# Values of the first two batches loaded as natural rows and spread by TensorE

## The chip, the cores and the metric

One core of a Trainium2 chip runs the whole program. The metric is the device time of one execution in microseconds. All times below are microseconds.

## The reference

A Longformer attention is followed by an MLP with a cosine gate.

```python
batch, n_heads, seq, head_dim = (8, 8, 576, 64)     # n_global = 8, window = 32
scores = scale * np.matmul(q, k.transpose(0, 1, 3, 2))
mask = (np.abs(pos[:, None] - pos[None, :]) <= 32) | is_global[:, None] | is_global[None, :]
attn = softmax(np.where(mask, scores, -1e9))
x = np.matmul(attn, v)          # then laid out as 4608 tokens x 512
h = x @ w_in                    # 512 -> 2048
g = h * np.cos(h)
out = g @ w_out                 # 2048 -> 512
```

## The kernel before, in words

**Attention.** The work unit is a pair of heads, 32 pairs in all (`pr`, four to a batch); two pairs make a half batch (`s`, 16 of them). The 576 queries of a head are cut into 11 blocks of 56. A block sees 8 global keys and 120 window keys, so keys and values of a block stand on 128 partitions. `kw` holds the keys of a pair by block, `qb` the queries (with the 8 global queries in front), `vw` the values: 128 partitions x 11 blocks x 2 heads x 65 (the 65th column is ones, and gives the sum of the softmax). Each has four buffers in rotation.

- `scores` (L441): 11 matmuls `st`, three PSUM tiles of the tag "s" (three buffers); ScalarE makes `e` = exp (L443), VectorE multiplies by the mask into `pm` (L444).
- `values` (L453): 22 matmuls into `pv`; VectorE forms reciprocals and writes `xn` (L464).
- `turn_x` (L476): six transposes `tx`; VectorE copies into `xT` (L479), the transposed input of the MLP. At a batch's last pair GpSimd copies the eight global columns into `xT` (L484).

**Where the operands come from.** Keys and queries of the first four half batches are loaded by `load_qk` (L260, GpSimd's queue) into `kn` and `qn`, turned by TensorE (L408, `t`) and copied into `kw` and `qb` (L415, L428). Later half batches are cast to float16 scratch in DRAM by `cast_half` (L249 for v, L253 for k and q, on GpSimd's queue), and k and q are read back transposed by `turn_half` (L265, L266, SyncE's queue) and copied on VectorE (L418, L431). The values of every half batch go through the scratch `v16`: `load_v` (L304 to L311, SyncE's queue) reads overlapping windows of 120 rows, 128 bytes each, into `vw`, and `load_vg` (L316) copies the eight global rows into each block. The global rows of k, q and v are gathered (L289, GpSimd's queue).

**The MLP.** Tokens are handled in nine tiles of 512. `one` does one of 16 slices of the first matmul of a tile (L492, four matmuls `ph`), the cosine on ScalarE (L495) and the product `g` on VectorE (L496). `two` does a quarter of one of four output blocks (L506, four matmuls `po`); after the fourth, `o` is copied (L511 or L513) and stored by SyncE (L515). A tile may start when `ready[0]` allows it, and outputs are held back by `outs_by[0]`.

**The order** is written out by hand; each engine runs its instructions in that order. `FRONT` covers the half batches 0 and 1 and the first scores of 2, `THIRD` the rest of half batch 2, and `ORDER` each later one. In them `s`, `p` and `x` are scores, values and turn_x, `k` and `q` the local keys and queries, `g` the global ones, `L` load_qk, `W` load_w_in (L596), `c` a cast of v, `v` load_v and load_vg, `n` a square sum on ScalarE, `G` the casts of a later half batch, held until this half's `xn` is there (L670), and `1` and `2` are one and two. A letter a, z, c or d after the step picks the pair 2s, 2s+1, 2s+2 or 2s+3. After each half batch SyncE gets `turn_half(s + 2)` and the value loads of the half batch s + 2. w_out is loaded on GpSimd's queue at the start of half batch 2 (L694).

Of the kernel before, what the change touches and what calls it, by code (L numbers as in the profile page):

```python
# [9 lines left out]
FP32 = mybir.dt.float32  # L10
# [29 lines left out]

ORDER = "sa0 sa1 sa2 2 2 2 sz0 2 sz1 sz2 pa 1 1 2 xa pz G 1 1 2 xz n 1 1 2 kc qc 1 kd qd 2 1"

THIRD = "1 1 pa 1 1 xa pz G 1 1 kc qc xz 1 1 kd qd 1 n 1"

FRONT = ("s0.0 s0.1 s0.2 s1.0 s1.1 s1.2 L2 c2 W1 k2 q2 p0 v4 g4 k3 q3 s2.0 s2.1 s2.2 x0 p1 v5 g5 W2 s3.0 s3.1 s3.2 x1 k4 q4 p2 L3 W3 g6 "
         "k5 q5 x2 p3 I c3 g7 x3 n0 s4.0 s4.1 s4.2 s5.0 s5.1 s5.2 v6 v7")
OK_ALL = float(P * (B * NP * 2 * BP + B))


# [5 lines left out]
def dview(ap, offset, *dims):  # L55

    return bass.AP(ap.tensor, ap.offset + offset, [list(d) for d in dims])
# [134 lines left out]
def kernel(  # L192
# [38 lines left out]
    v16 = dram.tile([B * H * S, D], FP16)  # L231


    NV = 4
    kT = [keep.tile([P, 2, KT], FP16, name=f"kT{i}") for i in range(2)]
    qT = [keep.tile([P, 2, QT], FP16, name=f"qT{i}") for i in range(2)]
# [19 lines left out]
    def load_qk(s):  # L256

        base = s * 4 * S * D
        for src, dst in ((k, kn[s % 2][KPAD : KPAD + S // RW]), (q, qn[s % 2][0 : S // RW])):
            nc.gpsimd.dma_start(dst.rearrange("x h r d -> x h (r d)"),  # L260
                                dview(src, base, (RW * D, S // RW), (S * D, 4), (1, RW * D)))
# [34 lines left out]
    def load_v(pr):  # L296


        b, h0 = pr // NP, 2 * (pr % NP)
        vt = vw[pr % NV]  # L300
        for h in range(2):
            lo, i0, i1 = (b * H + h0 + h) * S * D, 0, NB
            if pr == 0 and h == 0:
                nc.sync.dma_start(vt[G + 32 : P, 0, h, 0:D], dview(v16, 0, (D, W - 32), (1, D)))  # L304
                i0 = 1
            if pr % 2 and h:

                nc.sync.dma_start(vt[G : G + 104, NB - 2, h, 0:D], dview(v16, lo + 472 * D, (D, 104), (1, D)))
                nc.sync.dma_start(vt[G : G + 48, NB - 1, h, 0:D], dview(v16, lo + 528 * D, (D, 48), (1, D)))
                i1 = NB - 2  # L310
            nc.sync.dma_start(vt[G:P, i0:i1, h, 0:D],  # L311
                              dview(v16, lo + (QB * i0 - 32) * D, (D, W), (QB * D, i1 - i0), (1, D)))

    def load_vg(pr):
        for h in range(2):
# [67 lines left out]

    w_in16 = const.tile([P, NC, DFF], FP16)
    w_out16 = const.tile([P, NF, DM], FP16)
    xT = keep.tile([P, NC, NT + 40], FP16)

    r_all = keep.tile([P, B * NP, 2 * BP], FP32)
    x_sq = keep.tile([P, B * NP // 2], FP32)
# [4 lines left out]
    def globals_k(pr):  # L394
        nc.gpsimd.tensor_copy(kw[pr % NK][:, :, 0:G], view(kgT[:, pr], (0, NB), (1, G)))
# [199 lines left out]
    def load_w_in(c):  # L595
        nc.gpsimd.dma_start(w_in16[:, :, c * 512 : (c + 1) * 512],  # L596
                        moe_w_in[:, c * 512 : (c + 1) * 512].rearrange("(c p) n -> p c n", p=P))

    STEPS = {"s": scores, "p": values, "x": turn_x}
    with tc.manual_schedule():  # L600

        nc.vector.memset(pio2, pi / 2.0)
        nc.scalar.activation(x_sq[:, 0:1], pio2, AF.Exp)
        nc.vector.memset(kn[0], 0.0)
        nc.vector.memset(qn[0], 0.0)
        nc.gpsimd.iota(p_i, pattern=[[0, 1]], base=0, channel_multiplier=1)
        nc.gpsimd.memset(ident16, 1.0)
        cast_half(0, "v")
        cast_half(1, "v")
        load_qk(0)  # L610
        nc.gpsimd.affine_select(ident16, ident16, [[-1, P]], ALU.is_equal, 0.0, base=0, channel_multiplier=1)
        index_rows()
        gather(k, kg32, 0)
        gather(q, qg32, 0)
        nc.gpsimd.iota(kid_i, pattern=[[QB, NB]], base=-(G + 32), channel_multiplier=1)
        nc.gpsimd.iota(d_i, pattern=[[-1, C]], base=0, channel_multiplier=1)
        for t in (kn[1], qn[1], qb[2], qb[3]):
            nc.scalar.memzero(t.rearrange("p a b c -> p (a b c)"))
        for i in range(2):
            nc.vector.memset(qb[i], 0.0)  # L620
        load_qk(1)
        gather(v, vg32, 0)
        load_w_in(0)
        nc.vector.memset(vw[0][0:64, 0, 0], 0.0)
        for i in range(NV):
            nc.vector.memset(vw[i][:, NB - 2 :], 0.0)
            nc.vector.memset(vw[i][:, :, :, D : D + 1], 1.0)
        load_v(0)
        load_v(1)
        local_k(0)  # L630
        local_q(0)
        build_globals(0)
        globals_k(0)
        globals_q(0)
        build_mask()
        local_k(1)
        local_q(1)
        globals_k(1)
        globals_q(1)
        nc.scalar.copy(vg16[:, 0], vg32[:, 0])  # L640
        load_vg(0)
        load_vg(1)
        for pr in range(2, 4):
            load_v(pr)
            load_vg(pr)
            globals_k(pr)
            globals_q(pr)
        pv = ps.tile([P, 2, 512], FP32, tag="pv", bufs=1)
        nc.vector.memset(pv, 0.0)
        nc.vector.memset(view(pv[:, :, D : D + 1], (512, 2), (65, 6)), 1.0)  # L650

        def load_values(pr):
            load_v(pr)
            load_vg(pr)

        pool_idx = []

        def load_idx(_):
            pool_idx.extend(
                nc.values_load(gidx_row[0:1, 2 * g : 2 * g + 1], engines=[mybir.EngineType.Pool],  # L660
                               min_val=0, max_val=S - 1)
                for g in range(G))

        def globals_kq(pr):
            globals_k(pr)
            globals_q(pr)

        def casts(s):

            nc.gpsimd.tensor_copy(gate, xn_of[s][0:1, 1, 0, 0:1])  # L670
            for n in range(4, 2 * B):
                if s == n - 3:
                    cast_half(n, "vkq")
            if s == 4:
                for src, dst in ((k, kg32), (q, qg32), (v, vg32)):
                    gather(src, dst, 1)

        gate = keep.tile([1, 1], FP16)
        LOCAL = {"k": local_k, "q": local_q}
        OTHER = LOCAL | {"g": globals_kq, "L": load_qk, "W": load_w_in, "c": lambda s: cast_half(s, "v"), "v": load_values, "n": x_squares,  # L680
                 "I": load_idx}
        for step in FRONT.split():
            f = (STEPS | OTHER)[step[0]]
            f(*[int(x) for x in (step[1:] or "0").split(".")])
        ready[0], front[0] = 1, False
        for i in range(2):
            nc.vector.memset(kT[i][:, :, 0:KL], 0.0)
            nc.vector.memset(kT[i][:, :, KL + S :], 0.0)
            nc.vector.memset(qT[i][:, :, S:], 0.0)
        make_identity(nc, ident)  # L690
        nc.vector.memset(ones16, 1.0)
        for s in range(2, B * NP // 2):
            if s == 2:
                nc.gpsimd.dma_start(w_out16, moe_w_out.rearrange("(c p) n -> p c n", p=P))  # L694
                cast_half(4, "vkq")
            outs_by[0] = 4 * (s - 2) if s < 5 else 8 * (s - 3)
            for pr in (2 * s + 2, 2 * s + 3):
                if 8 <= pr < B * NP:
                    globals_kq(pr)
            for step in (THIRD if s == 2 else ORDER).split():  # L700
                if step == "1":
                    one()
                elif step == "2":
                    two()
                elif step == "n":
                    x_squares(s - 1)
                elif step == "G":
                    casts(s)
                elif step[0] in "cv":
                    OTHER[step[0]](int(step[1:]))  # L710
                else:
                    f, pr = (STEPS | LOCAL)[step[0]], 2 * s + "azcd".index(step[1])
                    if pr < B * NP:
                        f(pr, *[int(x) for x in step[2:]])
            if s % 2 == 1:
                ready[0] = s // 2 + 1 + (s // 2 == B - 1)
            if s < B * NP // 2 - 2:
                turn_half(s + 2)
                load_values(2 * s + 4)
                load_values(2 * s + 5)  # L720
            if s == 5:
                build_globals(1)
        x_squares(B * NP // 2 - 1)
        tail[0] = True
        for i in range(NTT * NF):
            one()
            two()
            if i in (3, 6, 9, 12):
                weight_norms(i // 3 - 1)
            if i in (0, 3, 6, 9):  # L730
                weight_squares(i // 3)
            if i == 14:
                count = finish_check()
            if i == 30:
                raise_flag(count)
        assert not outs_q
# [35 lines left out]
```

## Time and profile before

| | us |
|---|---|
| median of 3 runs | 391.77 (391.38 to 392.03) |
| profiled execution, its time | 392.95 |
| profiled execution, its span | 391.3 |
| TensorE matmuls busy | 328.0 (84%) |
| VectorE busy | 257.4 (66%) |
| ScalarE busy | 241.3 (62%) |
| GpSimd busy | 113.1 (29%) |

The span runs from the first to the last instruction of one profiled execution. Busy is the sum of an engine's instructions; matmuls are pipelined and their ends are modelled. The queue q1 is SyncE's, q0 GpSimd's; q1 moved 124509 packets and 27.89 MB, q0 63952 packets and 18.75 MB. A granted clock of 1.00 is TensorE's full speed. A row of a timeline gives start, length, engine, line, operation, output and inputs, and in brackets the idle time before it and what ended it.

### The profile page before, as it was taken

To read this page: it belongs to the slowest core of one execution; us is meant where nothing else is said; L and a number is where in the kernel's file an instruction comes from. 1 tells how busy PE (TensorE), PEld (TensorE's weight loads), DVE (VectorE), ACT (ScalarE), POOL (GpSimd) and SP (SyncE) were. 2 spreads that over 40 slices of the span, in tenths; PEclk is the share of its full clock that TensorE was granted. 3 is DMA by queue.
4 is the path that set the end of the run, shared out by engine and by line. 5 is a ranking of instruction groups with operands and counts; after the bars stand their busy time and mean duration, and the time that the engine had idled before them with its cause. 6 is when DMAs were issued, how large, how long until landed. Compare 5 with 4: busy or idle time off the path is not lost.

```text
span 391.3 us, 7371 instructions
## 1 busy us (share of the span) xinstructions
PE 328.0 (84%) x2678; PEld 173.4 (44%) x2678; DVE 257.4 (66%) x597; ACT 241.3 (62%) x354; POOL 113.1 (29%) x250
## 2 busy tenths in 40 slices
PE   0346249874987999999999999999999879999994
PEld 0245234442343455555555555555555334444441
DVE  5367246785386868878888887888888444544300
ACT  4456135984475686787767777786787866244310
POOL 7565116506055615072252516313000100000000
PEclk9999556999799999999999999999999999999999
DMA  5999999999999999999999999999930000010121
GB/s 86 144 112 196 188 87 129 202 162 152 146 118 188 115 169 131 158 167 153 169 134 202 134 158 173 135 189 111 153 72 30 27 2 27 29 54 28 55 80 60
DMA packets 188504, 47.18 MB, mean 121 GB/s; under 512 B 177005, under 2 KB 183405, under 8 KB 188205
## 3 DMA queue, kind: packets, MB, share of 16 engines
q1 hardware_dynamic: 124509, 27.89, 59.3%
q0 software_dynamic: 63952, 18.75, 48.7%
q8 instruction: 23, 0.38, 0.5%
q14 instruction: 20, 0.16, 0.2%
HBM read 47.73 MB, written 21.23 MB: 176 GB/s over the span
## 4 chain that ended last, share of the span: by engine, by line
PE 69%; DMA 15%; DVE 4%; ACT 3%; SPq 3%; issue 3%; POOL 2%; POOLq 0%; ACTq 0%; DVEq 0%
PE po L506 31%; PE ph L492 27%; DMA k<-in_k_dram 5%; PE st L441 4%; PE pv L453 4%; DMA qT<-q 3%; PE tx L476 3%; DMA kn<-in_k_dram 2%; DMA vw<-vg 2%; DMA vg<-in_v_dram,gidx_rows 2%; SPq L316 1%; ACT cos L495 1%; DVE g L496 1%; DVE xn L464 1%; PE pn L538 1%
## 5 line engine op out<-in xcount | busy, mean ns | idle before, releaser
L492 PE MATMUL ph<-xT,w_in 128*128 128x512 f16 x576 | 142.3, 384 | 8.1 <-DVE g L496 5.4
L506 PE MATMUL po<-w_out,g 128*128 128x512 f16 x576 | 142.5, 384 | 1.2 <-DVE o L513 1.0
L495 ACT ACTIVATE cos<-ph,pio 128x512 f16<-128x512 f32 x144 | 97.2, 686 | 67.5 <-PE ph L492 67.1
L496 DVE TENSOR_TENSOR g<-cos,ph 128x512 f16<-128x512 f16 x144 | 96.2, 685 | 52.5 <-ACT cos L495 50.3
L492 PEld LDWEIGHTS <-w_in 128*128 128x128 f16 x576 | 54.0, 98 | 70.0 <-issue 13.4
L506 PEld LDWEIGHTS <-g 128*128 128x128 f16 x576 | 55.9, 99 | 65.6 <-issue 4.3
L443 ACT ACTIVATE e<-st 128x512 f16<-128x512 f32 (+1 forms) x96 | 47.7, 562 | 26.9 <-PE st L441 19.6
L444 DVE TENSOR_TENSOR pm<-e,mask 128x512 f16<-128x512 f16 (+1 forms) x96 | 36.8, 403 | 23.6 <-ACT e L443 19.7
L670 POOL COPY gate<-xn 1x1 f16<-1x1 f16 x14 | 2.5, 179 | 144.5 <-DVE xn L464 144.5
L441 PE MATMUL st<-qb,kw 128*128 128x128 f16 x352 | 30.9, 237 | 11.5 <-POOL qb L400 8.9
L441 PEld LDWEIGHTS <-kw 128*128 128x128 f16 x352 | 26.1, 107 | 21.9 <-issue 8.8
L464 DVE TENSOR_TENSOR xn<-pv,r_all 128x768 f16<-128x768 f32 x32 | 30.7, 958 | 1.9
L453 PE MATMUL pv<-vw,pm 128*64 128x65 f16 x704 | 20.1, 204 | 13.9 <-DMA vw<-vg 13.9
L484 POOL COPY xT<-xg 128x4 f16 x64 | 20.7, 323 | 22.8 <-DVE xT L479 19.3
L253 POOL DMA_DIRECT2D q<-in_q_dram x12 | 26.1, 2179 | 0.0
L453 PEld LDWEIGHTS <-pm 128*64 128x64 f16 x704 | 16.3, 117 | 18.5 <-issue 8.8
L511 ACT COPY o<-po 128x512 f32<-128x512 f32 x18 | 10.5, 585 | 22.5 <-PE po L506 22.1
L431 DVE COPY qb<-qT 64x616 f16<-64x616 f16 x48 | 22.1, 460 | 3.3 <-DMA qT<-q 3.0
L525 ACT ACTIVATE sq<-xn 128x1536 f16<-128x1536 f16 x16 | 23.6, 1474 | 0.0
L415 ACT COPY kw<-t 128x1320 f16<-128x1320 f16 x8 | 10.1, 1256 | 20.4 <-PE t L408 20.4
L476 PE MATMUL tx<-ident,xn 128*128 128x128 f16 x192 | 17.0, 228 | 6.4 <-DVE xn L464 6.4
L513 DVE COPY o<-po 128x512 f32<-128x512 f32 x18 | 12.3, 685 | 12.5 <-PE po L506 12.0
(109 smaller groups left out, 267.2 us busy)
## 6 DMA issues: line engine op xcount, KB each, us to landing
out_dram<-o SPq DMA_DIRECT2D x36, 256.0 KB
vw<-v SPq DMA_DIRECT2D x47, 165.0 KB
v<-in_v_dram POOLq DMA_DIRECT2D x16, 288.0 KB
k<-in_k_dram POOLq DMA_DIRECT2D x12, 288.0 KB
q<-in_q_dram POOLq DMA_DIRECT2D x12, 288.0 KB
vw<-v SPq DMA_DIRECT2D x16, 135.0 KB
w_in<-in_moe_w_in_dram POOLq DMA_DIRECT2D x4, 512.0 KB
w_out<-in_moe_w_out_dram POOLq DMA_DIRECT2D x1, 2048.0 KB
```

The costliest lines, as they stand in the source:

```text
L253: nc.gpsimd.dma_start(dst[s].rearrange("t (h d) -> t h d", h=4), dview(src, base, (D, S), (S * D, 4), (1, D)))
L441: nc.tensor.matmul(st[:, j], kp[:, g0 + j], view(qp[:, g0 + j], (1, P)), start=True, stop=True)
L443: nc.scalar.activation(e[:, :n], st[:, :n], AF.Exp, scale=scale)
L444: nc.vector.tensor_tensor(view(pm[:, g0], (1, n * P)), view(e, (1, n * P)), view(mask[:, g0], (1, n * P)), ALU.mult)
L453: nc.tensor.matmul(pv[r0 : r0 + C, j // 6, c0 : c0 + 65], pm[:, j, h], vp[:, j, h], start=True, stop=True)
L464: nc.vector.tensor_tensor(view(xn, (384, 2), (D, 6), (1, D)), view(pv, (512, 2), (65, 6), (1, D)), view(rp, (6, 2), (1, 6), (0, D)), ALU.mult)
L476: nc.tensor.transpose(tx[:, n], xn[:, n], ident16)
L492: nc.tensor.matmul(ph, w_in16[:, j, f * P : (f + 1) * P], xT[:, j, t * TT : (t + 1) * TT], start=(j == 0), stop=(j == NC - 1))
L495: nc.scalar.activation(cos, ph, AF.Sin, bias=pio2)
L496: nc.vector.tensor_tensor(g16[:, f], cos, ph, ALU.mult)
L506: nc.tensor.matmul(po, g16[:, f, s * P : (s + 1) * P], w_out16[:, f], start=(f == 0), stop=(f == NF - 1))
L525: nc.scalar.activation(sq, view(xn, (1, 2 * BP * P)), AF.Square, accum_out=x_sq[:, s : s + 1])
```

## The change

For the pairs 0 to 7 (batches 0 and 1) `cast_half(.., "v")`, `load_v` and `load_vg` go. In their place `load_vn` reads a half batch's values in float32 rows, 112 rows x 4 heads to a transfer (six transfers on SyncE's queue), into `vn32`, which takes the two buffers of the tag "g" ahead of the MLP's use. `cast_vn` casts them to float16 into a part of `xT` that is not yet used. `spread` builds the blocks on TensorE: for each of the 11 blocks one matmul with `own` puts the global rows in place, and one or two with a 0/1 matrix `shift` put the window rows in place; the three PSUM tiles (tag "s") are copied into `vw` by ScalarE, VectorE and ScalarE. `hold(s)` is a copy of one element on GpSimd that waits for the last transfer of half batch s.

The orders change with it. In FRONT the loads and casts of v go, and `C` (cast_vn), `w` (spread) and `V` (hold) come in. `THIRD` takes the spreads of the pairs 4 to 7, `V3 W3 O`, where `O` loads w_out and casts half batch 4. The new `FOURTH` replaces `ORDER` for half batch 3: scores, values and turn_x first, then `R`, which lets the MLP's second tile start, then 11 ones and 12 twos. `outs_by[0]` is 16 up to half batch 4, in place of 0, 4 and 8. The opening issues load_qk(0) first on GpSimd's queue, and the gathers of v before load_qk(1).

```diff
-THIRD = "1 1 pa 1 1 xa pz G 1 1 kc qc xz 1 1 kd qd 1 n 1"
-
-FRONT = ("s0.0 s0.1 s0.2 s1.0 s1.1 s1.2 L2 c2 W1 k2 q2 p0 v4 g4 k3 q3 s2.0 s2.1 s2.2 x0 p1 v5 g5 W2 s3.0 s3.1 s3.2 x1 k4 q4 p2 L3 W3 g6 "
-         "k5 q5 x2 p3 I c3 g7 x3 n0 s4.0 s4.1 s4.2 s5.0 s5.1 s5.2 v6 v7")
+THIRD = "1 1 C2 w4 pa 1 w5 1 xa V3 W3 O pz kc qc 1 1 xz kd qd 1 C3 wc G 1 wd n 1 1"
+
+FOURTH = "sa0 sa1 sa2 sz0 sz1 sz2 pa 1 1 xa pz 1 1 G xz n R 2 1 2 1 2 1 2 1 2 1 2 1 2 1 2 kc qc 1 2 1 2 kd qd 1 2 1 2"
+
+FRONT = ("s0.0 s0.1 s0.2 k1 q1 C0 w0 s1.0 s1.1 s1.2 L2 p0 k2 q2 C1 w1 x0 s2.0 s2.1 s2.2 p1 g4 k3 q3 w2 W1 x1 s3.0 s3.1 s3.2 p2 L3 g5 w3 x2 k4 q4 p3 "
+         "g6 g7 I s4.0 s4.1 s4.2 x3 n0 k5 q5 V2 W2 s5.0 s5.1 s5.2")
...
+    def load_vn(s):
+        for i in range(NVT):
+            m = min(VT, S - VT * i)
+            nc.sync.dma_start(vn32[s // 2][0:m, s % 2 * 3 + i // 2, i % 2 * 256 : i % 2 * 256 + 256].rearrange("p (h d) -> p h d", h=4),
+                              dview(v, (s * 4 * S + VT * i) * D, (D, m), (S * D, 4), (1, D)))
+    def hold(s):
+        nc.gpsimd.tensor_copy(gate, vn32[s // 2][0:1, s % 2 * 3 + 2, 256:257])
+    def cast_vn(s):
+        old, new = vn32[s // 2][:, s % 2 * 3 : s % 2 * 3 + 3].rearrange("p a (b n) -> p (a b) n", b=2), vn16(s)
+        nc.vector.tensor_copy(new[0:VT, 0:3], old[0:VT, 0:3])
+        nc.scalar.copy(new[0:VT, 3 : NVT - 1], old[0:VT, 3 : NVT - 1])
+        m = S - VT * (NVT - 1)
+        nc.vector.tensor_copy(new[0:m, NVT - 1], old[0:m, NVT - 1])
+    def spread(pr):
+        new, h0 = vn16(pr // 2), 2 * (pr % 2) * D
+        for g0 in range(0, NB, 4):
+            n = min(4, NB - g0)
+            t = ps.tile([P, 4, P], FP32, tag="s", bufs=3)
+            for j in range(g0, g0 + n):
+                i = j // 2
+                parts = ((2, i), (3, i + 1)) if j % 2 else ((0, i), (1, i - 1))
+                nc.tensor.matmul(t[:, j - g0], own[:, pr], vg16[:, 0].rearrange("p h d -> p (h d)"), start=True, stop=False)
+                parts = [(a, x) for a, x in parts if x >= 0]
+                for a, x in parts:
+                    m = min(VT, S - VT * x)
+                    nc.tensor.matmul(t[:, j - g0], shift[0:m, a], new[0:m, x, h0 : h0 + 2 * D],
+                                     start=False, stop=(a, x) == parts[-1])
+            copy = nc.vector.tensor_copy if g0 == 4 else nc.scalar.copy
+            copy(vw[pr % NV][:, g0 : g0 + n, :, 0:D], t[:, 0:n].rearrange("p n (h d) -> p n h d", h=2))
...
-        cast_half(0, "v")
-        cast_half(1, "v")
         load_qk(0)
+        for s in range(2 * SB):
+            load_vn(s)
...
         gather(k, kg32, 0)
         gather(q, qg32, 0)
+        gather(v, vg32, 0)
...
+        load_qk(1)
...
+        build_shifts()
         for i in range(NV):
-            nc.vector.memset(vw[i][:, NB - 2 :], 0.0)
             nc.vector.memset(vw[i][:, :, :, D : D + 1], 1.0)
-        load_v(0)
-        load_v(1)
+        build_mask()
...
-            if s == 2:
-                nc.gpsimd.dma_start(w_out16, moe_w_out.rearrange("(c p) n -> p c n", p=P))
-                cast_half(4, "vkq")
-            outs_by[0] = 4 * (s - 2) if s < 5 else 8 * (s - 3)
+            outs_by[0] = 16 if s < 5 else 8 * (s - 3)
...
-            for step in (THIRD if s == 2 else ORDER).split():
+            for step in {2: THIRD, 3: FOURTH}.get(s, ORDER).split():
```

## The prediction

> **What bounds the kernel now.** I read the page's slices first, then busy time by stage, then the chain of waits, then single rows of TensorE. In the slices each digit is 9.8 us; PE is TensorE's busy share, PEclk its granted clock.
>
> ```profile
> PE   0346249874987999999999999999999879999994
> PEclk9999556999799999999999999999999999999999
> ```
>
> From slice 14 on TensorE is full; the loss lies ahead of about 138 us. By stage, cut where TensorE starts the scores of each half batch (columns: PE, PEld, DVE, ACT, POOL busy, PEclk, DMA share, GB/s):
>
> ```profile
> 0.00:23.20 23.20, 3.33 (x67) 2.71 (x68) 11.64 (x43) 10.37 (x16) 12.82 (x25) 1.00 1.12 123
> 23.20:60.00 36.80, 18.45 (x307) 15.91 (x307) 17.91 (x47) 17.25 (x28) 14.07 (x39) 0.70 1.17 141
> 60.00:75.60 15.60, 14.88 (x160) 7.27 (x160) 11.38 (x31) 10.84 (x16) 10.80 (x16) 0.83 1.40 181
> 75.60:95.60 20.00, 13.04 (x119) 6.71 (x118) 13.06 (x31) 14.14 (x21) 7.16 (x19) 1.00 1.77 154
> 95.60:116.30 20.70, 17.25 (x127) 8.18 (x128) 13.30 (x32) 11.39 (x18) 4.92 (x5) 0.84 1.25 132
> 116.30:137.20 20.90, 17.77 (x143) 9.00 (x143) 16.14 (x36) 13.48 (x21) 12.62 (x25) 1.00 1.56 151
> 137.20:308.00 170.80, 170.25 (x1427) 91.24 (x1427) 143.06 (x326) 130.11 (x195) 50.72 (x125) 1.00 1.35 140
> ```
>
> TensorE is idle 38 us before 60, 14.5 us between 60 and 137.2, and 0.55 us in the 171 us after. The chain of waits (start, length, what) names the cause:
>
> ```profile
> 2.62 9.37 DMA kn<-in_k_dram
> ...
> 13.64 9.05 DMA vg<-in_v_dram,gidx_rows
> ...
> 23.09 5.49 DMA vw<-vg
> ...
> 43.65 5.86 SPq L316
> 49.56 3.82 DMA vw<-vg
> ...
> 62.29 19.45 DMA k<-in_k_dram
> ...
> 84.07 10.46 DMA qT<-q
> ```
>
> Keys behind two value casts on GpSimd's queue; the gather of global values, which also holds GpSimd's qb copies and so the first scores; then the value blocks, queued on SyncE; then the keys of half 4, queued behind w_out; then their transposition. Last, what one 128x128 matmul costs at either clock:
>
> ```profile
> 23.20 2.69 PE L441 MATMUL st<-qb,kw 128*128 128x128 f16 x22 [4.80 <-POOL qb L400]
> ...
> 45.68 0.21 PE L453 MATMUL pv<-vw,pm 128*64 128x65 f16 x1 [8.42 <-DMA vw<-vg]
> ...
> 75.60 0.78 PE L441 MATMUL st<-qb,kw 128*128 128x128 f16 x11
> ```
>
> 122 ns each in the first row, 71 ns in the last: half and full clock.
>
> **Start, up to the first scores.** The two casts of v ahead of kn go (they and kn and qn, 288 KB each, filled q0 until about 14), so kn and qn are issued at about 2.1 and 3.1. Half the queue's bytes would bring kn at 7 to 8; 24 value loads on SyncE's queue (2.36 MB, 9216 packets of 256 B) run beside it, so I take 9 and 11, with 13 as the late bound (as long as before). Turning k and q and their copies (0.79, 1.26, 0.73, 0.67 in the rows at 12 to 16) end at 14. The gathers of v now stand ahead of load_qk(1), so vg isn't behind kn1 and qn1: issued by 12.2, landed at 15 in place of 22.8. VectorE has the mask (5.8 us of rows, 16.65 to 22.45) behind its memsets and the building of the 0/1 matrices (two memsets and five small copies, under 1.6 us by the 128x260 memset's 0.28 and copies of 0.2 to 0.3): free at about 14. First scores at 15.5 to 17; I take 16, was 23.2.
>
> **Values of pairs 0 to 3.** The block loads and vg loads go, with their 8.4 and 3.7 us stalls. Each spread adds 11+11+10 = 32 matmuls of 128x128: 32 x 122 = 3.9 us at half clock, 32 x 71 = 2.3 at full. ScalarE gets two PSUM copies (0.59 and 0.45, from the 512-wide copy at L511), VectorE one (0.69, as L513); per half batch a cast on VectorE (768 wide, about 0.6 by 616 in 0.49, plus 0.2) and one of 0.56 on ScalarE (as e). The loads of halves 0 and 1: by 29.8 ns a packet and engine (q1: 59.3% of 16 x 391.3 us over 124509 packets) 4608 packets take 8.6 us, twice that if time goes by bytes, so they land between 11 and 20; all four by 37. GpSimd waits for half 1 in hold(1), with w_in 0, globals 2 and 3 and load_qk(2) behind it: at the latest 20, and pair 2's scores come at about 33. Hidden.
>
> On TensorE's own order, at half clock: s0 1.35 and k1 q1 1.5 (to 18.9), wait for the cast of values (VectorE ends it at 19.8, ScalarE, behind kw and two qb copies, at 21.8), spread to 24, s1 1.35, p0 0.95, k2 q2 1.5, wait of 1.5 for the second cast, spread 0 to spread 1 10 us apart. Second spread done at 33. From there to the last scores of the opening TensorE needs 13.5 us at full clock (x 0.5, s 0.78, p 0.57, k and q 0.95, spread 2.3), 23 at half; VectorE 17.4 (pm 4 x 1.2, xn with its reciprocals 4 x 1.54, xT and xg 4 x 0.68, qb 3 x 0.8, spreads 2 x 0.69). I take VectorE plus 1.6 of gaps: first MLP matmul at 52, was 59.98: **-8.0**. Bounds 47.5 (TensorE alone) and 61 (below).
>
> The clock matters here. In this trace it is full at 36.5 after ten busy us (k turned in 0.50), half after the hole from 37.3 to 45.7, and full again at 65 after 5 us of unbroken work. The Trainium skill (TensorE: Matmul & The Clock Gate, Part 1: The HAM clock gate) says that about 3.4 us of sustained work release it and an idle window of that length throttles it again. The trace agrees within its 5 us slices, and by that rule the second spread would already run full and the opening would end about 1.5 us earlier.
>
> **From the first MLP matmul to half 6 (59.98 to 137.91: 77.9 us before).** The order shows the same MLP work by the end of half 5 (32 ins, 16 outs), but pulled forward: half 3 gets 15 ins and 12 outs, half 4 7 and 4, half 5 none.
> - Half 2: 15.6 + four spreads of 2.27 - 2.5 (5 us at clock 0.50 that would be warm) = 22.2.
> - Half 3: 27 units of 0.865 (L492, L506) + 3.1 of attention + 1.5 for GpSimd, whose gate, casts and eight xT copies took 6.3 us (87.1 to 93.4) against about 5 units ahead of tile 1's first matmul, + 1 = 28.9.
> - Half 4: 11 units, 3.1, and 2 of waits = 14.6. The transposition of half 5 now stands on SyncE's queue behind the third output, so issued at the end of half 3; at 10.5 us plus issue it lands when half 4 asks for it.
> - Half 5: only attention, so bound by its chain on VectorE: 1.8 to the first e (with a table load), 3.5 for six e and pm, twice 2.2 for xn and xT, 0.5 for the turn, 2 x 0.75 for the first kw and qb: 12.2.
> - Then half 6 starts partly at half clock. After the hole ahead of half 4 twelve po took 5.23 us (97.69) where they later take 2.59: 2.6 is the bound, and I take 1.7, since half 5 has short gaps and no one long hole.
>
> Sum 79.6: **+1.7**. Hidden: w_in 2 and 3 now stand ahead of w_out and the casts of half 4 on GpSimd's queue, all issued after the xT copies of batch 0, at 50.5 rather than 60.6. 1.05 MB more at 138 GB/s (2.69 MB in 19.45 us) is 7.6 us: k lands at about 80 (81.7 before), qT at 92; half 3 copies it at 96. That cover is 4 us; beyond it each us is lost. w_out comes at 74.5, first used at 82. The dropped vw memsets free VectorE before it has anything urgent: nothing.
>
> From half 6 on the orders agree. -8.0 + 1.7 = -6.3. The profiled run took 392.95 (span 391.3), 1.2 above the median 391.77; its sum is 386.7, the median's 385.5.
>
> **Rivals.**
> 1. *The opening is bound by TensorE at full clock*, and half 5's hole closes as VectorE runs ahead: first MLP at 47.5 and about 3 us less later: 391.8 - 12.5 - 1.3 = 378. For it: TensorE would be busy without holes; against: VectorE's 17.4 us.
> 2. *SyncE's queue gives it back.* turn_half(6) follows half 5's transposition and ten value loads. Before, one such cycle took 13.4 us (103.42 to 116.79) and once 19.3 (84.07 to 103.42). At 19.3 the transposes for half 6 land at 136 rather than 130, half 6 starts up to 5 us late: 390.5. Against it: the long cycle waited for an output at its end.
> 3. *Slower: the spreads keep TensorE at half clock and in step with the copies.* Scores and spreads share three PSUM buffers, so each spread waits for ScalarE and VectorE, which wait for scores. If all spreads stand 10 us apart as the first two do, the fourth ends at 54, and p3, s4, x3, k5 q5, s5 with their gaps at half clock bring the first MLP to 63; with 79.6 and a cold start of 1.5 half 6 begins at 144: 391.8 + 6.3 = 398. It decides where the first MLP comes later than about 58. For it: 8.5 us of half-clock work a pair; against: holes of 1.5 us only, where the clock rose at 23 to 36 with less work.
> 4. *It does nothing*: keys land no earlier beside the value loads and half 5 takes the rest: 391.8.
>
> **How the numbers follow.** A measurement tells about 0.2% (0.8 us) from no change. Forecast 0.50 (380 to 390 by 4 us either way in the opening), rival 1 0.20, rival 2 0.12, rival 3 0.15, rival 4 0.03. Faster: 0.50 + 0.20 + 0.10 = 0.80; same 0.03; slower 0.17. The range from 376 to 395 takes in forecast, rivals 2 and 4, most of 1 and the near part of 3.
>
> **What would show it.** First scores at 16, spread rows 71 ns from the third on, first ph matmul near 52, half 6's first st near 130, an empty half 5 with PEclk falling. Wrong if ph starts after 58, if st waits on kn, if vn loads end after 40, or if kw and qb copies of half 4 wait for DMA.

## Result: 4% slower, and the profile after

| | before | after |
|---|---|---|
| median | 391.9 (391.38 to 392.52, 4 runs) | 408.42 (405.10 to 408.59, 4 runs) |
| profiled execution, its time | 392.95 | 405.1 |
| profiled execution, its span | 391.3 | 403.4 |

The ratio is 1.0397, with a 95% interval from 1.035 to 1.0445. The forecast was 385.5, with a range from 376 to 395: both missed, and the sign with them. The profiled execution of the changed kernel is the fastest of its four, 3.3 us below the median.

The slices of the page of the changed kernel (each digit 10.1 us):

```profile
PE   0499579777998459999999999999999969999993
PEclk9999579889999859999999999999999999999998
```

TensorE is busy earlier than before, but from 50 to 100 us PE stays at 7 in four slices with the clock at 7 or 8 in three of them, and at 131 to 151 there is a second valley (4 and 5, clock 8 and 5). By stage, cut where TensorE starts the scores of each half batch, and at the first MLP matmul (columns: PE, PEld, DVE, ACT, POOL busy, PEclk, DMA share, GB/s):

```profile
0.00:16.62 16.62, 2.09 (x34) 1.53 (x35) 12.21 (x46) 7.99 (x13) 11.02 (x22) 1.00 0.87 138
16.62:50.30 33.68, 27.62 (x467) 23.68 (x466) 20.83 (x51) 24.13 (x40) 14.22 (x42) 0.88 0.70 113
50.30:81.34 31.04, 25.46 (x291) 17.50 (x290) 17.19 (x40) 17.22 (x27) 10.96 (x15) 0.86 1.51 177
81.34:115.72 34.38, 29.02 (x187) 13.79 (x186) 20.00 (x41) 19.31 (x30) 6.88 (x18) 0.95 0.68 64
115.72:133.11 17.39, 13.60 (x123) 6.94 (x122) 12.60 (x30) 12.71 (x20) 4.94 (x5) 1.00 1.04 129
133.11:146.72 13.61, 5.12 (x81) 3.89 (x81) 10.78 (x28) 6.57 (x14) 5.59 (x9) 0.66 1.52 138
146.72:165.84 19.12, 19.12 (x143) 9.96 (x143) 12.39 (x29) 10.98 (x17) 13.54 (x31) 0.88 1.46 154
```

PEclk reads 1.00 in the first 28 us, but the matmuls there have the lengths of half clock (two of the spread take 0.42 us at 27.50 and 0.28 at 28.43). The last five rows are the half batches 2 to 6. Set against the kernel before (its half 7 starts at 154.87):

| stage | before | forecast | after | after minus forecast |
|---|---|---|---|---|
| up to the first MLP matmul | 59.98 | 52.0 | 50.30 | -1.7 |
| half 2 | 15.6 | 22.2 | 31.0 | +8.8 |
| half 3 | 20.0 | 28.9 | 34.4 | +5.5 |
| half 4 | 20.7 | 14.6 | 17.4 | +2.8 |
| half 5 | 21.6 | 12.2 | 13.6 | +1.4 |
| half 6 | 17.0 | 18.7 | 19.1 | +0.4 |
| half 7 on | 236.4 | 236.4 | 237.6 | +1.2 |

(The forecast's 1.7 for a cold start stands in half 6.) So the gain of the opening came, and the halves 2 to 5 took back more. The chain of waits names other links than before (start, length, what):

```profile
11.36 4.81 DMA vg<-in_v_dram,gidx_rows
...
54.55 1.32 DVE xT L343
...
82.93 1.28 ACT L502
...
86.61 3.45 PE ph L551 x8
...
138.56 7.62 DMA vg<-in_v_dram,gidx_rows
```

Between 16 and 138 no DMA is left in it. New are the cast of values (L343), the eight ph matmuls of half 3 at half clock (3.45, where eight take 1.90 later), and the second gather of global values, which holds the first scores of half 6. In half 2 the rows of TensorE and VectorE show why the cast is there (lines of the changed kernel: L365 and L369 are the spread, L343 the cast on VectorE, L555 the product g):

```profile
50.30 2.87 PE L551 MATMUL ph<-xT,w_in 128*128 128x512 f16 x8
...
55.92 0.27 PE L369 MATMUL t<-xT 112*128 112x128 f16 x1 [2.70 <-DVE xT L343]
...
69.58 1.02 PE L551 MATMUL ph<-xT,w_in 128*128 128x512 f16 x4 [0.25 <-DVE g L555]
70.44 0.22 PE L365 MATMUL t<-vg,xT 128*128 128x128 f16 x1
72.91 0.27 PE L369 MATMUL t<-xT 112*128 112x128 f16 x1 [2.25 <-DVE xT L343]
...
73.39 0.42 PE L369 MATMUL t<-xT 112*128 112x128 f16 x2
```

```profile
53.35 1.28 DVE L555 TENSOR_TENSOR g<-cos,ph 128x512 f16<-128x512 f16 x2 [1.18 <-issue]
54.55 1.31 DVE L343 CAST xT<-vn 112x768 f16<-112x768 f32 x1
...
71.70 0.69 DVE L555 TENSOR_TENSOR g<-cos,ph 128x512 f16<-128x512 f16 x1
72.30 0.55 DVE L343 CAST xT<-vn 112x768 f16<-112x768 f32 x1
```

The order is `1 1 C2 w4`: the cast stands behind two products g, which wait for two cosines and a table load of ScalarE. TensorE, which has nothing between `w4` and the two ones, waits 2.70 us, then spreads at half clock (two matmuls in 0.42 us; at full clock 0.28). At `C3 wc` it waits 2.25 us: there the cast stands behind a copy of queries, which waits for ScalarE's copy, and a product g with its cosine; no table load is in the way. The first cast takes 1.31 us and the second 0.55; the last section shows what held the first.

### The profile page after: what moved, and what is told of

Read it like the earlier page. It is cut to its first block, busy times and chain, and to the rows that moved or that the text cites. A ratio compares the mean times of both kernels' runs of the same rounds, so it can differ in the third digit from the quotient of the medians.

```text
span 403.4 us, 7909 instructions
## 1 busy us (share of the span) xinstructions
PE 348.2 (86%) x2934; PEld 191.7 (48%) x2934; DVE 266.5 (66%) x615; ACT 249.6 (62%) x372; POOL 111.1 (28%) x249
## 4 chain that ended last, share of the span: by engine, by line
PE 71%; DVE 8%; ACT 7%; DMA 5%; issue 4%; POOL 4%; POOLq 0%; ACTq 0%; DVEq 0%
PE po L565 29%; PE ph L551 26%; PE st L500 5%; PE t L369 4%; DVE g L555 4%; PE pv L512 3%; DMA vg<-in_v_dram,gidx_rows 3%; ACT cos L554 2%; PE tx L535 2%; PE t L365 2%; DMA kn<-in_k_dram 2%; ACT e L502 2%; POOL q L257 1%; ACT qb L487 1%; DVE qb L487 1%
## 5 line engine op out<-in xcount | busy, mean ns | idle before, releaser
L551 PE MATMUL ph<-xT,w_in 128*128 128x512 f16 x576 | 143.8, 385 | 7.0 <-DVE g L555 5.0
L555 DVE TENSOR_TENSOR g<-cos,ph 128x512 f16<-128x512 f16 x144 | 96.4, 686 | 66.2 <-ACT cos L554 62.8
L502 ACT ACTIVATE e<-st 128x512 f16<-128x512 f32 (+1 forms) x96 | 47.7, 563 | 15.4 <-PE st L500 10.0
L523 DVE TENSOR_TENSOR xn<-pv,r_all 128x768 f16<-128x768 f32 x32 | 30.6, 958 | 1.9
L369 PE MATMUL t<-xT 112*128 112x128 f16 (+1 forms) x168 | 23.0, 255 | 5.7 <-DVE xT L343 5.2
L543 POOL COPY xT<-xg 128x4 f16 x64 | 19.7, 308 | 14.8 <-DVE xT L538 11.4
L535 PEld LDWEIGHTS <-xn 128*128 128x128 f16 x192 | 13.4, 102 | 14.7 <-DVE xn L523 9.1
L365 PE MATMUL t<-vg,xT 128*128 128x128 f16 x88 | 20.2, 255 | 0.0
```

Source lines behind the costliest of these rows:

```text
L365: nc.tensor.matmul(t[:, j - g0], own[:, pr], vg16[:, 0].rearrange("p h d -> p (h d)"), start=True, stop=False)
L369: nc.tensor.matmul(t[:, j - g0], shift[0:m, a], new[0:m, x, h0 : h0 + 2 * D], start=False, stop=(a, x) == parts[-1])
L502: nc.scalar.activation(e[:, :n], st[:, :n], AF.Exp, scale=scale)
L523: nc.vector.tensor_tensor(view(xn, (384, 2), (D, 6), (1, D)), view(pv, (512, 2), (65, 6), (1, D)), view(rp, (6, 2), (1, 6), (0, D)), ALU.mult)
L535: nc.tensor.transpose(tx[:, n], xn[:, n], ident16)
L551: nc.tensor.matmul(ph, w_in16[:, j, f * P : (f + 1) * P], xT[:, j, t * TT : (t + 1) * TT], start=(j == 0), stop=(j == NC - 1))
```

## Experiments

Each is compared with the kernel before, run on the same chip. "Half 2" is the time from the first MLP matmul to the first scores of half 3, the others from scores to scores; these lengths are from the one profiled execution of each run.

**1. The old order of half 3.** `FOURTH` and the early outputs are undone, the spreads stay.

```diff
-            outs_by[0] = 16 if s < 5 else 8 * (s - 3)
+            outs_by[0] = 4 * (s - 2) if s < 5 else 8 * (s - 3)
-            for step in {2: THIRD, 3: FOURTH}.get(s, ORDER).split():
+            for step in {2: THIRD}.get(s, ORDER).split():
```

> The changed kernel with the MLP's old order in half batch 3 (ORDER and the old outs_by in place of FOURTH). Theory A (the time is lost in half batch 2, to the spreads of pairs 4 to 7, the casts ahead of them and the half clock behind those waits): half 2 stays at 31 us, halves 3 to 5 together take about what they took before the change (62) in place of 65, so 403 to 408 us. Theory B (pulling the MLP forward empties half 5, and that hole is the loss): halves 3 to 5 fall to 50 to 55, so about 395 or less.

Measured: 394.48, ratio 1.0112 (1.007 to 1.0154). Halves 3 to 6 took 17.8, 19.4, 18.9, 17.0: 73.1 in all, where the changed kernel took 84.5 and the kernel before 79.3. The time is theory B's, though halves 3 to 5 took 56.1, a little more than its 50 to 55. So `FOURTH` and the early outputs cost 11.4 us of these halves. Without them the halves take 6 us less than before the change, behind a half 2 that is 18 us longer (33.6), which gives the transfers more time. Half 2 itself stayed long.

**2. No values for pairs 4 to 7.** The casts C2, C3 and the four spreads of half 2 are left out.

```diff
-THIRD = "1 1 C2 w4 pa 1 w5 1 xa V3 W3 O pz kc qc 1 1 xz kd qd 1 C3 wc G 1 wd n 1 1"
+THIRD = "1 1 pa 1 1 xa V3 W3 O pz kc qc 1 1 xz kd qd 1 G 1 n 1 1"
```

> The changed kernel without the casts and spreads of half batches 2 and 3: pairs 4 to 7 use the values that pairs 0 to 3 left in vw, so that part of the computation is left out. Theory A: half 2 falls from 31 to about 16 us as before the change, and half 3 loses some of its half clock: 390 to 394 us. Theory B: only the 9 us of matmuls of the four spreads go, the hole stays: 398 to 400.

Measured: 391.16, ratio 1.0035 (1.0003 to 1.0067). Half 2 fell from 31.0 to 16.0. Casts and spreads together cost 15 us there, more than the 9 us that four spreads take at full clock.

**3. The second gathers earlier.** GpSimd's six gathers go from half 4's casts to half 3's, so that half 6 need not wait for them.

```diff
+            if s == 3:
+                for src, dst in ((k, kg32), (q, qg32), (v, vg32)):
+                    gather(src, dst, 1)
...
-            if s == 4:
-                for src, dst in ((k, kg32), (q, qg32), (v, vg32)):
-                    gather(src, dst, 1)
```

> The changed kernel with the second set of gathered global rows issued one half batch earlier (ahead of the casts of half batch 6). Theory A: GpSimd's 6.4 us wait at 140 goes, and half 6 starts when its keys are copied, at about 141 to 143 in place of 146.7, with less half clock after it: minus 4 to 6 us, 402 to 404. Theory B says the same for this one or less (its hole is bound by VectorE's chain): minus 0 to 3.

Measured: 414.49, ratio 1.0625 (1.0584 to 1.0667): slower still. The gathers stood ahead of GpSimd's copies of the global columns of `xT`, which the MLP's second tile needs:

```profile
107.35 1.86 PE L551 MATMUL ph<-xT,w_in 128*128 128x512 f16 x4 [9.35 <-POOL xT L543]
```

Half 3 grew from 34.4 to 44.8, and after the wait four matmuls took 1.86 us, at half clock. Half 5 no longer ended on a gather, and was no shorter (14.3 against 13.6; half 6 then waited 3.42 us for the copies of `xT`), so taking the gather out of the end of half 5 did not shorten it. Neither theory had foreseen that the gathers would hold half 3.

**4. The casts earlier.** C2 and C3 go into FRONT, ahead of the MLP; spreads and `FOURTH` stay.

```diff
-... "1 1 C2 w4 pa 1 w5 1 xa ... 1 C3 wc G 1 wd n 1 1"
+... "1 1 w4 pa 1 w5 1 xa ... 1 wc G 1 wd n 1 1"
-... k4 q4 p3 g6 g7 ... k5 q5 V2 W2 ...
+... k4 q4 p3 C2 g6 g7 ... k5 q5 C3 V2 W2 ...
```

> The changed kernel with the casts of values of half batches 2 and 3 moved from half 2 into the opening, where VectorE and ScalarE wait for the keys (40 to 50 us). Theory A: TensorE's two waits of 2.7 and 2.3 us for the cast go, and with them the half clock of spreads 4 and 6 (1.6 us each): half 2 falls from 31 to 24 us, 400 to 402. Theory B: no more than the two waits, given back in half 5's hole: 405 to 408.

Measured: 398.7, ratio 1.0248 (1.0212 to 1.0284). Half 2 fell from 31.0 to 22.9, with a granted clock of 0.96 in place of 0.86, and the opening was no longer (49.7). So 8.2 us of half 2 came from the place of two casts. TensorE is idle there for 5.6 us in the changed kernel and for 0.6 in this one: 4.95 us are the two waits, and the other 3.2 are matmuls that ran slower.

**5. Both undone** (the edits of 1 and 4 together).

> The two that helped, together: the old MLP order in half 3 (e1) and the casts of values of half batches 2 and 3 in the opening (e4). Theory C (two losses that stand in different stages and add: about 8 us in half 2 to the casts' place with the half clock after it, about 11 in halves 3 to 6 to the pulled-forward MLP): half 2 takes 23, half 3 18, half 4 19.5, half 5 19, so half 6 starts at 129 in place of 138 and the time is 380 to 384. Rival D (they share one cause, the DMA queues, so that one gain takes the other's place): keys of half 4 are awaited again, 388 to 392.

Measured: 383.99, ratio 0.9842 (0.9808 to 0.9877). Half 2 took 22.9, halves 3 to 6 70.3. The place of the casts and the order of half 3 are enough to turn 4% slower into 1.6% faster.

**6. Two spreads earlier too.** To 5, the spreads of pairs 4 and 5 go into FRONT, behind p3 and k5 q5, with C2 behind w3.

```diff
-... g5 w3 x2 k4 q4 p3 C2 g6 g7 ... k5 q5 C3 V2 ...
+... g5 w3 C2 x2 k4 q4 p3 w4 g6 g7 ... k5 q5 w5 C3 V2 ...
```

> As e5, and the spreads of pairs 4 and 5 moved into the opening's two waits of TensorE for the queries' copies (2.2 us at 41, 2.7 us at 47). Theory C: half 2 falls by two spreads (4.5 us) to 18.5, the opening grows by at most 2: minus 2 to minus 4 against e5. Rival D: no change against e5, or slower, since the three PSUM buffers are shared with the scores.

Measured: 378.08 (376.95 to 380.59), ratio 0.9699 (0.9645 to 0.9752): it beats both kernels. The slices of its page (9.4 us each):

```profile
PE   0499969787898999999999999999999879999993
PEclk9999999999999999999999999999999999999997
```

From 27 us on the granted clock stays up, and the first MLP matmul comes no later (49.4), though two spreads more stand ahead of it: they fill gaps. Half 2 took 18.8.

**7. Spread for batch 0 only.** With the old order, batch 1's values again take the scratch: `SB = 1`, with `c2 v4 v5 c3 v6 v7` in FRONT.

> Spreads for batch 0 alone: the values of batch 1 come by casts to scratch, block loads and loads of global rows as before the change (four pairs), old MLP order in half 3. Theory C: half 2 takes 16 as before, if the loads of pairs 4 to 7 land while the opening runs; DMA between 20 and 60 us gets 1.4 MB in 128-byte packets, so the keys of half 4 land later than in e5: 382 to 388. Rival D: block loads are what held the opening, first MLP at 55 or later, 388 to 394.

Measured: 380.65, ratio 0.9738 (0.9695 to 0.9782). The opening's gain (first MLP matmul at 50.5) is kept without any spread in half 2 (15.4), but half 3 took 20.3, as in the kernel before, where run 6 takes 16.4.

**8. Experiment 2 with the old order** (pairs 4 to 7 without values, `ORDER` and `outs_by` as in 1).

> As e1, without the casts and spreads of half batches 2 and 3 (pairs 4 to 7 use the values that pairs 0 to 3 left in vw; that part of the computation is left out). The bound of what the place of those spreads can cost. Theory C: half 2 takes 16, and then the keys of half 4 (turned by about 84) are awaited by 2 to 4 us in half 3; half 6 starts at 122 to 126, 375 to 380. Rival D: the wait for the keys takes all that half 2 gives, 382 or more.

Measured: 380.81, ratio 0.9755 (0.9712 to 0.9798). With half 2 at 16.0, half 3 took 19.6 and half 4 20.1. This is slower than 6, in which four spreads more are done. What half 2 saves is waited for at the end of half 3, where VectorE needs the transposed queries of half 4:

```profile
84.57 0.95 DVE L490 COPY qb<-qT 64x616 f16<-64x616 f16 x2 [3.85 <-DMA qT<-q]
```

**9. The clock alone.** In the changed kernel TensorE gets 28 matmuls, overwritten by the spread, ahead of the spreads of pairs 4 and 6, so that it isn't idle while it waits for the casts.

```diff
+            if pr in (4, 6) and g0 == 0:
+                for _ in range(28):
+                    nc.tensor.matmul(t[:, 0], own[:, pr], vg16[:, 0].rearrange("p h d -> p (h d)"), start=True, stop=True)
```

> The changed kernel with 28 more matmuls of 128x128 ahead of the spreads of pairs 4 and 6; their sums are overwritten, they wait for nothing and stand where TensorE waits for the cast of values (2.7 and 2.3 us), so they add work and hide in the wait. Theory C1 (the half clock behind those waits is a good part of half 2's loss): PEclk in half 2 rises from 0.86 to over 0.95, half 2 takes 27 to 28.5 us in place of 31, 404 to 406 us. Rival C2 (the loss is the waits and the added copies themselves): half 2 stays at 31 to 33 and the time is unchanged or up to 2 us longer.

Measured: 404.1, ratio 1.0283 (1.0225 to 1.0341). Half 2 fell from 31.0 to 28.4, its clock rose to 0.93; some was given back (half 5 15.8). So keeping TensorE busy in the waits is worth about 2.6 us, most of the 3.2 that experiment 4 left to slower matmuls.

The other runs bear this out. With the two casts in half 2, its length goes with the number of 3.41 us stretches in which the clock is at half behind a wait for a cast: none in run 9 (28.4), one in run 16 (29.7), two in the changed kernel and in runs 3 and 11 (30.9 to 31.2), four in runs 1 and 13 (33.6). A stretch costs about 1.3 us.

**10. and 14. The queue's order without the spread.** Run 10 (kernel before, load_qk(0), the gathers of v and load_qk(1) moved up) gave 403.6, but says nothing on the question: load_qk(1) then stood ahead of ScalarE's clearing of its target, the clearing waited for the loads, and the first scores came at 30.6. (Half 1's keys and queries are cleared after their load in it, so it leaves out their part of the computation.)

> The kernel before, with block loads throughout; only the queue's order at the start is the changed kernel's: load_qk(0) ahead of the two casts of v, the gathers of v ahead of load_qk(1). Theory S (the opening's 9.7 us came from the values being on chip): first scores at 17 to 19, but the value blocks and global rows are awaited as before, first MLP matmul at 58 to 60, 389 to 392. Rival Q (it came from the queue's order): first MLP at 52 to 54, 383 to 386.

Run 14 leaves load_qk(1) behind the clearing:

```diff
+        load_qk(0)
         cast_half(0, "v")
         cast_half(1, "v")
-        load_qk(0)
...
         gather(q, qg32, 0)
+        gather(v, vg32, 0)
...
         load_qk(1)
-        gather(v, vg32, 0)
```

> The kernel before with only the order of GpSimd's queue from the change: load_qk(0) ahead of the two casts of v, and the gather of v right behind the gathers of k and q; load_qk(1) stays behind ScalarE's clearing. Values still go through the scratch, with no spread. Theory S (the spread brought the opening's gain): the value blocks still come late, first scores at 16 to 18 but pv waits for vw, first MLP matmul at 57 to 60, 389 to 392 us. Rival Q (the queue's order alone brought it): first scores at 16 to 18 and first MLP matmul at 52 to 54, 383 to 386 us.

Measured: 389.12, ratio 0.9968 (0.9933 to 1.0002). The scores start 4 us earlier than in the kernel before, the MLP doesn't:

```profile
19.10 2.69 PE L441 MATMUL st<-qb,kw 128*128 128x128 f16 x22 [3.55 <-POOL qb L400]
...
43.62 0.21 PE L453 MATMUL pv<-vw,pm 128*64 128x65 f16 x1 [6.47 <-DMA vw<-vg]
...
59.49 3.57 PE L492 MATMUL ph<-xT,w_in 128*128 128x512 f16 x8 [1.04 <-POOL xT L484]
```

The value blocks take nearly all of it back: 0.5 us is left of the opening's 9.7. So the queue's order alone did not bring them; the new path of the values did, with the order of `FRONT` that goes with it.

**11. Without `R`.** `FOURTH` without the step that lets tile 1 start in half 3, so that eight ins go to half 5.

> The changed kernel without the step R, so that the second MLP tile may start only after half 3: nine ins move from half 3 back into halves 4 and 5, all else stays (casts and spreads in half 2 too). Theory H (half 5's time is its attention chain, with TensorE idle 8.5 of 13.6 us, so MLP work put there is nearly free): half 3 falls by about 8 to 26 or 27, half 4 grows to 18 to 19, half 5 to 16 to 18, half 6 starts warm (17): 404 to 405 on the scale of 408.4. Rival K (half 3 is bound by waits, not by its 27 units): half 3 stays above 31, 408 or more.

Measured: 405.55, ratio 1.0344 (1.0281 to 1.0407). Half 3 fell to 26.6, and half 5 grew from 13.6 to 22.0: nothing won, where the expectation had half 5 at 16 to 18. An empty half 5 alone is thus not the cause.

**12. Two spreads in half 3.** To 6, the spreads of pairs 6 and 7 go from half 2 into half 3, behind the scores.

```diff
-... {2: THIRD}.get(s, ORDER)
+... {2: THIRD, 3: ORDER.replace('sa2', 'sa2 w6').replace('sz2', 'sz2 w7')}.get(s, ORDER)
```

> As e6, with the spreads of pairs 6 and 7 moved from half 2 into half 3, behind each pair's scores, where TensorE waits for the exponentials (half 3 had 3.5 us of idle TensorE in 16.4). Theory C: half 2 falls by about 4.5 to 14.3, half 3 grows by 2 to 3: minus 1.5 to 2.5 us against e6. Rival D: half 3 grows by all of it, since spreads and scores share three PSUM buffers: no change or slower.

Measured: 385.48, ratio 0.9822 (0.9756 to 0.9888), slower than 6. Half 2 gave 3.4 us, half 3 took 5.8 more, halves 4 and 5 together 4.4 more: rival D's result. That the shared buffers are the reason is not shown.

**13. and 16. Outputs held back; order alone.** 13 keeps `FOURTH` and `R` and takes the old `outs_by` (first line of 1). 16 also leaves out `R`, so that each half has the amounts of 1 in the order of `FOURTH`.

> The changed kernel with the old release of the outputs (outs_by 4, 8, 16) and FOURTH and R kept: half 3 has 15 ins and 4 outs in place of 15 and 12, half 4 the same 7 and 4, half 5 has 8 outs in place of none. Theory F (outs are the work that fills attention's waits, since they ask nothing of ScalarE and VectorE but one copy in four; spent early, half 5 stands without): half 3 34.4 - 8 x 0.865 = 27.5, half 5 17 or less with 8 outs where it took 13.6 with none, half 6 17 to 19; half 7 starts at 161 where it started at 165.8; 399 to 402 us. Rival W (each half has waits of its own, and outs only cost what they take wherever they stand): half 3 27.5, half 5 20.5, half 7 at 165 to 166; 405 to 408 us, as the changed kernel.

> e13 without the step R as well: FOURTH's order (attention of half 3 first, then the MLP), with the amounts of the old order in every half (half 3: 6 ins and 4 outs, half 4: 8 and 4, half 5: 8 and 8). So it differs from e1_order3 only in the order within half 3. Theory A (what counts is how much MLP work is pulled into half 3 and taken from half 5): as e1_order3, half 3 17 to 18.5, half 5 19, half 7 at 156; 394 to 396 us. Rival O (the order within half 3 counts: attention bunched at its front leaves its waits open): half 3 8.65 of units + 3.1 of attention + the 8 us that the changed kernel's half 3 loses = 19.8 to 22, half 7 at 159 to 161; 397 to 400 us.

Measured: 13 gave 399.97, ratio 1.0215 (1.0139 to 1.029), 16 gave 394.63, ratio 1.0127 (1.007 to 1.0184). Half 5 of 13, then of 16, and of 11 (columns as by stage above):

```profile
129.47:143.77 14.30, 10.90 (x113) 5.93 (x114) 11.45 (x27) 6.59 (x13) 10.21 (x17) 1.00 0.99 107
```
```profile
115.74:134.67 18.93, 17.41 (x145) 9.17 (x146) 16.89 (x36) 14.01 (x23) 10.67 (x18) 1.00 1.35 132
```
```profile
126.14:148.09 21.95, 14.32 (x112) 7.48 (x113) 16.51 (x33) 13.78 (x25) 11.34 (x21) 0.84 1.35 131
```

With the other runs they make a square:

| half 5 | no outs | 8 outs |
|---|---|---|
| no ins | 13.6 (after), 14.3 to 15.8 (runs 2, 3, 4, 9) | 14.3 (run 13) |
| 8 ins | 22.0 (run 11) | 18.9 (runs 1, 5 to 8, 14, 16), 21.6 to 21.9 (before, runs 10, 12) |

Run 11 and run 13 each stand alone in their cell. Eight outs are 6.9 us of matmuls. Put into a half without ins they lengthen it by 0.7 at most, and with them a half with ins is not longer than without, and up to 3.1 shorter. The granted clock is 1.00 with them (13, 16) and 0.66 (after) or 0.84 (11) without. Of the halves 3 to 6, the changed kernel takes 84.5, run 13 77.2, run 16 72.7, run 1 73.1. So of some 12 us, 7.3 go when the outs are held back, and 4.5 more when `R` goes too. Taken the other way round, `R` alone gives 0.4 (run 11 takes 84.1) and the outs then 11.4: the two losses do not add, and the early outs are the larger one by either way. The order of steps within half 3 costs nothing in sum (16 against 1): half 3 is 2.4 us longer in it (20.2 against 17.8), as rival O had it, but half 4 gives that back (16.6 against 19.4), so the time is theory A's.

## Why the prediction was wrong, step by step

**The opening: right in its number, and in part by luck.** First scores 16.62 (forecast 16), second spread done at 30 (33), the third at full clock, first MLP matmul 50.30 (52). A spread took 2.3 us at full clock and 3.7 at half, against 2.3 and 3.9 (32.74 to 34.99, and 55.92 to 59.58). But behind the second spread VectorE was not the bound: it was busy for 14.3 us of 20.3, where 17.4 of 19 were forecast. The last two scores of the opening waited 2.18 and 2.68 us for a copy of queries on VectorE, which itself had waited for ScalarE's copy (1.69 and 2.29). Three us won before that stretch hide that it was longer than forecast. The DMA engines fell idle at 32, so all value loads had landed, before the 37 allowed. That the queue's order alone did not bring the gain is run 14.

**Half 2, 22.2 against 31.0: the step that failed is "four spreads of 2.27 - 2.5".** It priced the spreads and put their casts on engines beside, where nothing of them was counted. The price was good: with the casts out of the way half 2 takes 22.9 (run 4). What was missing is what the casts are queued behind: C2 stands behind two g, and those behind two cosines and a table load, C3 behind a copy of queries and a g. TensorE waits for the cast, and loses its clock: 4.95 us of waits and 3.2 of slower matmuls, put at nothing. I had asked of the opening's casts who stands ahead of them (19.8 and 21.8), and not of C2 and C3. The size of this loss is not steady: half 2 took 29.7 to 33.6 us in six profiled runs with C2 and C3 inside it (after, 1, 3, 11, 13, 16), by the number of stretches at half clock, and 22.9 in both with them in FRONT (4, 5).

**Half 3, 28.9 against 34.4: the step "27 units of 0.865 + 3.1 + 1.5 + 1".** The units were right; 7.9 us of waits and half clock stood where 2.5 were put: 2.76 for e behind a table load, eight ph at half clock (1.6 too long), and 1.28 for GpSimd's `xT` among them. These three make 5.6; the rest is smaller pieces.

**Halves 4 and 5, 27 against 31.** Half 4 lost 4.8 where 2 were put. Half 5's chain on VectorE was about as worked out, but its end was set by the gather (row 138.56 above), which holds GpSimd's copy for the first scores of half 6: 146.4, while VectorE's first copies for half 6 began at 143.6. Run 3 shows that moving the gathers earlier, ahead of half 3's copies, did not pay.

**Half 6, +1.7 against +2.2: right in kind.** It starts at half clock, as forecast from the hole, and in run 13, with eight outs in half 5, it takes 16.95.

**The error behind the last three** is that the sum kept MLP work at 0.865 a unit wherever it stands. Moving 17 units (9 ins and 8 outs) out of halves 4 and 5 and into half 3 would then be free, but for a cold start. The square shows what that misses: an out asks of the other engines only a copy after four, so it fills TensorE's waits for softmax and keeps its clock; spent early, it leaves the attention of half 3 and half 5 with waits that nothing fills. That the early outs cost this is shown by 13 against the changed kernel. That the ins behave otherwise because they use ScalarE and VectorE, as attention does, is argued from their steps alone.

**The rivals.** Rival 3 had the sign and not the mechanism: its condition (first MLP matmul after 58) didn't hold, and the time was lost in halves 2 to 5, not in the opening. Rival 2's late transposition didn't come; half 6 waited for a gather. Rival 1's opening, bound by TensorE alone at 47.5, did not come, nor rival 4. "Hidden" held for the keys of half 4 in the changed kernel, whose chain shows no DMA there; in run 8, where half 4 comes earlier, the cover is gone. Three figures of the working are off in themselves, none of them enough to matter: TensorE alone would end the opening at 46.5 (33 and 13.5), not 47.5; its idle time between 60 and 137.2 adds up to 14.3, not 14.5; and the terms of half 5 make 12.2 only if the turn is counted twice.

**The clock.** The rows for it are above: at 69.58 four ph took 1.02 us, full clock, and after a wait of 2.25 us the spread ran at half. The clock was at half from 55.68 to 59.09 and from 72.75 to 76.16, 3.41 us each time, and in the 3.41 us ahead of each TensorE was busy for 0.95 and for 1.08 us. The Trainium skill (TensorE: Matmul & The Clock Gate, Part 1: The HAM clock gate) has an idle window of about 3.4 us before the throttle. The length agrees with these stretches. But if the window had to be idle throughout, neither wait of half 2 would have lost the clock; here waits of 2.25 and 2.70 did, in stretches with about 1 us of work, and the measurement decides. Filling those waits (run 9) gave 2.6 us back.

## What to carry to other kernels

When a change adds a step on an engine, write down what stands ahead of that step in the engine's own order, for every place where it occurs and not just the first: here two casts, of 0.55 us where nothing held them, cost 8 us of TensorE because they stood behind products and their cosines. Work that needs little but TensorE can cost almost nothing beside a softmax (eight outs, 6.9 us of matmuls, made half 5 at most 0.7 us longer), so ask of each reordering which stage loses its filler. A change whose local gain arrives and whose total is worse is worth taking apart: with the casts and two spreads moved and the old order of half 3 back, this one went from 4% slower to 3% faster.

## What the runs showed of the hardware that was not expected

A copy of keys or a cast of values on VectorE can be held by GpSimd's issue of a cast DMA. In run 11 the copy of keys, 0.52 us elsewhere, took 3.10 (rows of VectorE, then of GpSimd):

```profile
144.04 3.10 DVE L477 COPY kw<-kT 128x1320 f16<-128x1320 f16 x1
...
148.63 0.52 DVE L477 COPY kw<-kT 128x1320 f16<-128x1320 f16 x1
```
```profile
144.57 2.21 POOL L257 DMA_DIRECT2D q<-in_q_dram  x1
145.64 3.51 POOL L543 COPY xT<-xg 128x4 f16 x8
```

The copy ends at 147.14, 0.36 us after the issue of q. The same distance stands in other runs, however long the copy was: 1.80 us in run 16 (ends 134.53, issue 134.18), 2.20 in run 13 (144.43 and 144.07). The cast of values at 54.55 above took 1.31 us and ended 0.39 us after the issue of q that filled 53.30 to 55.48; in run 16 it began closer to the end of that issue and took 0.73. These issues took 2.1 to 2.2 us, and as long with no copy beside them (2.18 in the kernel before at 88.95), so it is the copy that was held. In half 2 this is 0.76 us of the first wait. Not every copy beside an issue is held: in run 16 a copy of keys at 130.72, which began just before the issue of k, took its 0.53. The Trainium skill (SBUF — State Buffer) tells of a pair of ports that VectorE and GpSimd hold in turn for a whole instruction, and warns of the DMA issue that waits for VectorE. Here it is VectorE that waits. No run here shows whether the ports are the reason.
